# V of a batch as one 4 MB tile in 32 KB rows, P·V in four column tiles, P replicated by GpSimd, O placed by its summing matmuls, eight batches in one loop

## The chip, the cores and the metric

The kernel runs on one core of one Trainium2 chip. The metric is the device time of one execution in microseconds (us); lower is better. Executions of the kernel before agree within 0.3%: 193.13 to 193.42 us in its first three runs.

"Packet" below means one contiguous row that one of the core's 16 DMA engines moves. Each has a start and a duration in the trace, and where the text gives packet durations they are medians or means over such records. In profile lines PE is TensorE, PEld its weight loads, DVE VectorE, ACT ScalarE, POOL GpSimd and SP SyncE; a q behind a name is that engine's sequencer, and L595 is line 595 of the kernel. The trace does not say which of the 16 engines moved a packet.

## The reference

One decode step of a transformer block for 8 batches. Layernorm, a query of 32 heads of 128, attention over the last 2048 positions of a K and V cache with 8 KV heads (four query heads share one), an output projection and a residual, then an MLP block with its own layernorms.

```python
W = min(4096, max(256, Sk // 4))                       # 2048
q = (x @ wq).reshape(B, Sq, Hq, Dh).transpose(0, 2, 1, 3)
k = jnp.repeat(k_cache[:, :, Sk - W:, :], rep, axis=1)  # rep = 4
v = jnp.repeat(v_cache[:, :, Sk - W:, :], rep, axis=1)
scores = jnp.einsum("bhqd,bhkd->bhqk", q, k) * (Dh ** -0.5)
p = _softmax(scores, axis=-1)
o = jnp.einsum("bhqk,bhkd->bhqd", p, v)
return o.transpose(0, 2, 1, 3).reshape(B, Sq, Hq * Dh) @ wo
# ... then h = x + attention, and h + MLP(h)
```

All values are bf16. K and V of one batch are 4.19 MB each (8 heads x 2048 positions x 128 x 2 bytes), 67.1 MB for eight batches; the weights bring the total to 79.2 MB, each byte read once.

## The kernel before

K and V come in tiles of four KV heads (`GL = 4`). With `C = 64`, a tile's partition 4p+g (one of the 128 rows of the memory on the chip) holds 64 positions of head g: one row of 16 KB. A transfer is 32 x 4 rows, 2 MB. All transfers of K, V and weights are issued in order by SyncE.

```python
# [cut] one transfer a tile, K and V alike
src = cache[b, GL * gq:GL * (gq + 1), W0:SK, :].rearrange("g (p c) d -> p g (c d)", c=C)
e.dma_start(dst, src).then_inc(sem_slot[slot], 16)      # dst: one slot of 128 partitions x 16 KB
```

TensorE transposes K (64 groups of 16), multiplies by q, ScalarE takes the exponential in two halves, P is transposed in 16 matmuls a batch and masked. Then P·V runs in two column tiles of 64, each matmul 512 columns wide and covering four quarters of the positions at once, so that VectorE has to pick and add the quarters:

```python
        def pe_PV(e, v, parts=(0, 1)):
            # [cut] waits
            vq = slots[:, slot, :].rearrange("p (q c d) -> p c q d", q=NT, d=DH)
            for cc in range(CC):
                # [cut]
                a = cc % 2
                ins = e.matmul(pv_ps[gq][64 * a:64 * (a + 1), :].rearrange("p (q d) -> p q d", d=DH),
                               pT_sb[:, gq, cc, :], vq[:, cc, :, :],
                               start=(cc < 2), stop=(cc >= CC - 2),
                               tile_position=(0, 64 * a), skip_group_check=True)

        def dve_O1(e, v):
            # [cut]
            w = mrl[:, b % 2, gq, :]
            ins = e.tensor_scalar(o_sum[:, gq, :], pv_ps[gq][:, 0:DH], w[:, 0:1], None, ALU.mult)
            for q in range(1, NT):
                chain(e, ins, "dve_self", dve_self)
                ins = e.scalar_tensor_tensor(o_sum[:, gq, :], pv_ps[gq][:, q * DH:(q + 1) * DH], w[:, q:q + 1],
                                             o_sum[:, gq, :], ALU.mult, ALU.add)
```

## Time and profile before

| | before |
|---|---|
| time, median of 3 runs | 193.36 us |
| span of the profiled run | 191.5 us |
| PE, DVE, ACT busy | 76%, 55%, 47% |
| bytes moved | 79.3 MB |
| DMA rate in the middle of the run | about 431 GB/s |

The slice rows of the page cut the span into 40 equal parts. A digit of `DMA` is the busy share of the 16 DMA engines in tenths, and the row below is what they moved:

```profile
DMA  6999999999999999999999999999999999999991
GB/s 221 438 431 428 428 421 431 433 431 424 431 428 428 435 431 438 431 428 431 426 428 438 431 435 430 428 431 428 428 438 431 431 431 431 431 431 401 418 398 54
```

From the second slice to the last but one the engines move 398 to 438 GB/s. The part on the queues (packets, MB, time of the packets as a share of 16 engines' span) and the chain that ended last say the same: the last long piece of it is weights landing.

```profile
q1 hardware_dynamic: 6832, 79.18, 97.5%
...
DMA 11%; SPq 3%; PE 1%; DVEq 0%; DVE 0%; issue 0%
```

97.5% of 191.5 us is 186.7 us: each of the 16 engines spent that long on its packets, on average. Rows of 16 KB (K, V) took 611 ns in the median, rows of 32 KB (wq) 1213 ns: the same rate.

The groups that the change touches (busy us, mean ns of one, then the idle time before them and what ended it) and the transfers (KB each, median us from issue to landing):

```profile
L595 PE MATMUL b<-slots,pT_sb 128*64 128x512 bf16 x128 | 16.5, 384 | 1.2 <-PEq L454 1.2
L595 PE MATMUL misc<-slots,pT_sb 128*64 128x512 bf16 x128 | 15.3, 382 | 0.6 <-PEq L454 0.6
L577 DVE TENSOR_TENSOR pT_sb<-kT_ps,maskT 128x1024 bf16<-128x1024 bf16 x16 | 10.5, 685 | 10.7 <-PE kT_ps L489 10.7
L611 DVE SCALAR_TENSOR_TENSOR o_sum<-misc,mrl,o_sum 128x128 f32<-128x128 f32 x24 | 8.4, 351 | 0.8
```

```profile
slots<-in_A_k_cache_dram SPq DMA_DIRECT2D x16, 2048.0 KB, 14.2
slots<-in_A_v_cache_dram SPq DMA_DIRECT2D x16, 2048.0 KB, 16.5
slots<-in_A_wq_dram SPq DMA_DIRECT2D x1, 4096.0 KB, 12.3
```

### The profile page before, as it was taken

The page shows a single profiled execution, that of the slowest core. Times are in us where ns is not written, and L with a number is a line of the kernel's source. Part 1 is how long each engine was busy: PE and PEld are TensorE (multiplying, and loading weights), DVE is VectorE, ACT ScalarE, POOL GpSimd, SP SyncE. Part 2 cuts the span into 40 slices and gives each one's busy share as a digit, 9 for nine tenths or more (in the row PEclk, how much of TensorE's full clock was granted, in tenths as well). Part 3 has the DMA queues.
Part 4 walks back from the last instruction along what each step waited for, and adds up shares of the span by engine and source line. Part 5 has one row for each costly group of instructions (what it writes and reads, how often), then busy time and mean ns, then how long its engine had stood idle before and what let it go on. Part 6 is the DMA issues. An engine that isn't in the chain of part 4 may idle for free. (4 is left out here: it accounts for less than half of the span.)

```text
span 191.5 us, 4850 instructions
## 1 busy us (share of the span) xinstructions
PE 145.9 (76%) x2028; PEld 99.3 (52%) x2028; DVE 105.2 (55%) x287; ACT 90.3 (47%) x113; POOL 1.9 (1%) x14
## 2 busy tenths in 40 slices
PE   2027998796899869886989688968896888776854
PEld 0003876582857455645564547553655465343842
DVE  6401757464268474747474747565665657585141
ACT  3301676862656265536643564447344835406041
POOL 4000000000000000000000000000000000000000
PEclk9999999999699999999999999999999999999555
DMA  6999999999999999999999999999999999999991
GB/s 221 438 431 428 428 421 431 433 431 424 431 428 428 435 431 438 431 428 431 426 428 438 431 435 430 428 431 428 428 438 431 431 431 431 431 431 401 418 398 54
DMA packets 6857, 79.31 MB, mean 414 GB/s; under 512 B 688, under 2 KB 704, under 8 KB 2368
## 3 DMA queue, kind: packets, MB, share of 16 engines
q1 hardware_dynamic: 6832, 79.18, 97.5%
q8 instruction: 6, 0.10, 0.2%
q14 instruction: 3, 0.02, 0.0%
q10 hardware_dynamic: 16, 0.01, 0.0%
HBM read 79.18 MB, written 0.01 MB: 414 GB/s over the span
## 5 line engine op out<-in xcount | busy, mean ns | idle before, releaser
L496 ACT ACTIVATE kT_sb<-kT_ps 128x1024 bf16<-128x1024 bf16 x64 | 64.6, 1028 | 67.3 <-PE kT_ps L473 66.9
L473 PE MATMUL kT_ps<-perm_b,slots 128*128 128x128 bf16 x1024 | 68.5, 223 | 22.9 <-PEq L454 22.8
L473 PEld LDWEIGHTS kT_ps<-perm_b,slots 128*128 128x128 bf16 x1024 | 60.8, 100 | 33.7 <-issue 33.7
L500 DVE COPY kT_sb<-kT_ps 128x1024 bf16<-128x1024 bf16 x64 | 43.3, 688 | 27.1 <-PE kT_ps L473 27.1
L516 PE MATMUL S_ps<-kT_sb,qcur 128*32 128x512 bf16 x256 | 22.5, 387 | 0.8 <-PEq L454 0.8
L546 ACT ACTIVATE P_sb<-S_ps,mtile 128x1024 bf16<-128x1024 f32 x16 | 17.8, 1115 | 2.6 <-DVE mtile L537 2.5
L595 PE MATMUL b<-slots,pT_sb 128*64 128x512 bf16 x128 | 16.5, 384 | 1.2 <-PEq L454 1.2
L577 DVE TENSOR_TENSOR pT_sb<-kT_ps,maskT 128x1024 bf16<-128x1024 bf16 x16 | 10.5, 685 | 10.7 <-PE kT_ps L489 10.7
L595 PE MATMUL misc<-slots,pT_sb 128*64 128x512 bf16 x128 | 15.3, 382 | 0.6 <-PEq L454 0.6
L526 DVE TENSOR_REDUCE mtile<-S_ps 128x1 f32<-128x512 f32 x8 | 5.5, 692 | 13.6 <-PE S_ps L516 13.6
L595 PEld LDWEIGHTS misc<-slots,pT_sb 128*64 128x64 bf16 x128 | 6.8, 109 | 8.4 <-issue 3.6
L595 PEld LDWEIGHTS b<-slots,pT_sb 128*64 128x64 bf16 x128 | 6.2, 109 | 9.2 <-issue 5.7
L516 PEld LDWEIGHTS S_ps<-kT_sb,qcur 128*32 128x32 bf16 x256 | 5.3, 93 | 8.3 <-issue 4.2
L489 PEld LDWEIGHTS kT_ps<-ident_b,P_sb 128*128 128x128 bf16 x128 | 7.2, 98 | 4.1 <-issue 4.1
L489 PE MATMUL kT_ps<-ident_b,P_sb 128*128 128x128 bf16 x128 | 8.7, 219 | 0.6 <-PEq L454 0.6
L611 DVE SCALAR_TENSOR_TENSOR o_sum<-b,mrl,o_sum 128x128 f32<-128x128 f32 x24 | 8.4, 351 | 0.8
L611 DVE SCALAR_TENSOR_TENSOR o_sum<-misc,mrl,o_sum 128x128 f32<-128x128 f32 x24 | 8.4, 351 | 0.8
L395 PE MATMUL S_ps<-slots,xlnT 128*8 128x512 bf16 x32 | 3.6, 626 | 5.7 <-DMA slots<-in_A_wq_dram 5.7
L412 DVE TENSOR_SCALAR q_sb<-S_ps 128x512 bf16<-128x512 f32 x1 | 0.7, 692 | 9.1 <-PE S_ps L395 9.1
L626 DVE CAST o_all<-misc 16x128 bf16<-16x128 f32 x7 | 2.0, 279 | 6.4 <-PE misc L620 6.3
L395 PEld LDWEIGHTS S_ps<-slots,xlnT 128*8 128x8 bf16 x32 | 1.0, 117 | 7.4 <-issue 7.4
L657 ACT ACTIVATE opl<-kT_ps 128x224 bf16<-128x224 f32 x1 | 1.2, 1182 | 6.6 <-PE kT_ps L649 6.6
(104 smaller groups left out, 82.5 us busy)
## 6 DMA issues: line engine op xcount, KB each, us to landing
slots<-in_A_k_cache_dram SPq DMA_DIRECT2D x16, 2048.0 KB, 14.2
slots<-in_A_v_cache_dram SPq DMA_DIRECT2D x16, 2048.0 KB, 16.5
slots<-in_A_wq_dram SPq DMA_DIRECT2D x1, 4096.0 KB, 12.3
slots<-in_A_wo_dram SPq DMA_DIRECT2D x1, 2048.0 KB, 30.7
slots<-in_B_w_dram SPq DMA_DIRECT2D x2, 896.0 KB, 32.0
slots<-in_A_wo_dram SPq DMA_DIRECT2D x1, 1024.0 KB, 32.5
slots<-in_A_wo_dram SPq DMA_DIRECT2D x2, 512.0 KB, 33.7
slots<-in_B_w_dram SPq DMA_DIRECT2D x1, 1024.0 KB, 25.7
```

The lines of the kernel that those rows point to most:

```text
L395: ins = e.matmul(S_ps[32 * j:32 * j + B, k, :], xlnT[:, kc * B:(kc + 1) * B], wq_v[:, kc, n0:n0 + 512], start=(kc == 0), stop=(kc == KC - ...
L473: ins = e.matmul(kT_ps[t % 2][:, c * 128:(c + 1) * 128], src[:, c * 128:(c + 1) * 128], perm_b[:, :], is_transpose=True)
L489: ins = e.matmul(kT_ps[half][:, c * 128:(c + 1) * 128], P_sb[:, half * W // 2 + c * 128:half * W // 2 + (c + 1) * 128], ident_b[:, :], is_ ...
L496: e.activation(kT_sb[:, i % NKT, 0:W // 2], kT_ps[i % 2][:, 0:W // 2], ACT.Copy).then_inc(sem_Elo, 1)
L500: e.tensor_copy(kT_sb[:, i % NKT, W // 2:W], kT_ps[i % 2][:, W // 2:W]).then_inc(sem_Ehi, 1)
L516: ins = e.matmul(S_ps[32 * gl:32 * (gl + 1), 0, :], qcur[:, GL * gq + gl, o:o + 32], kv[:, gl, :, :], start=(t == 0), stop=(t == 2 * NT - ...
L526: ins = e.tensor_reduce(mtile[:, 2, 0:1], S_ps[:, 0, :], AX.X, ALU.max)
L546: e.activation(P_sb[:, half * W // 2:(half + 1) * W // 2].rearrange("r (k g) -> r k g", g=GL), s_rep, ACT.Exp, bias=mtile[:, j, 0:1], scal ...
L577: e.tensor_tensor(pT_sb[:, :, half * hc:(half + 1) * hc, :].rearrange("p a c (g x) -> p (c g) a x", g=GL), kT_ps[half][:, 0:W // 2].rearra ...
L595: ins = e.matmul(pv_ps[gq][64 * a:64 * (a + 1), :].rearrange("p (q d) -> p q d", d=DH), pT_sb[:, gq, cc, :], vq[:, cc, :, :], start=(cc < ...
L611: ins = e.scalar_tensor_tensor(o_sum[:, gq, :], pv_ps[gq][:, q * DH:(q + 1) * DH], w[:, q:q + 1], o_sum[:, gq, :], ALU.mult, ALU.add)
L626: e.tensor_copy(o_all[:, gq, b, :], pv_ps[gq][0:GL * R, OT]).then_inc(sem_oT, 1)
```

## The change

Its intent is to shorten the work behind P·V. V of a batch becomes one tile of all eight heads, partition 8p+g, rows of 32 KB (128 positions). P is replicated eight times (an exponential for two copies, GpSimd for the rest), transposed in 32 matmuls instead of 16, and masked, so that P·V runs in four column tiles of 32 and adds up the quarters by itself. One scaling replaces eight VectorE steps, and four small fp32 matmuls a batch both add up the heads and put O in place. All eight batches now run in one TensorE loop. The core of the diff:

```diff
-NS = 10
+NS = 9
+            e.memset(P_rep[:], 0.0).then_inc(sem_rep, 2)
+            for b in range(NB):                                   # GpSimd
+                e.wait_ge(sem_exp, b + 1)
+                for x in range(2):
+                    e.tensor_copy(P_rep[:, x, :]..., <P_two read four times over>).then_inc(sem_rep, 1)
 # [cut] transfers
-                if kind in "kv":
-                    b, gq = divmod(t, 2)
-                    cache = A_k_cache if kind == "k" else A_v_cache
-                    src = cache[b, GL * gq:GL * (gq + 1), W0:SK, :].rearrange("g (p c) d -> p g (c d)", c=C)
-                    e.dma_start(dst, src).then_inc(sem_slot[slot], 16)
+                if kind == "k":
+                    # [cut] as before, 32 x 4 rows of 16 KB
+                if kind == "v":
+                    if t:
+                        e.wait_ge(sem_PV, t)
+                    src = A_v_cache[t, :, W0:SK, :].rearrange("g (p c) d -> p g (c d)", c=2 * C)
+                    e.dma_start(v_loop, src).then_inc(sem_v, 16)
+                if kind == "vl":      # V of the last batch, in two halves
+                    src = A_v_cache[NB - 1, :, W0:SK, :].rearrange("g (p x c) d -> x p g (c d)", x=2, c=C)[t]
+                    e.dma_start(dst, src).then_inc(sem_vl[t], 16)
 # [cut] P·V
-                ins = e.matmul(pv_ps[gq][64 * a:64 * (a + 1), :]..., pT_sb[:, gq, cc, :], vq[:, cc, :, :], ...
-                               tile_position=(0, 64 * a), skip_group_check=True)
+                        ins = e.matmul(pv_ps[32 * q:32 * (q + 1), :],
+                                       pT_sb[:, x, c, 32 * q:32 * (q + 1)],
+                                       v[:, k * DH:(k + 1) * DH], start=(x == 0 and c == 0), stop=(x == 1 and c == CT - 1),
+                                       tile_position=(0, 32 * q), skip_group_check=True)
 # [cut] O
-            ins = e.tensor_scalar(o_sum[:, gq, :], pv_ps[gq][:, 0:DH], w[:, 0:1], None, ALU.mult)
-            for q in range(1, NT):
-                ins = e.scalar_tensor_tensor(...)
+            e.tensor_scalar(o_sum[:, :], pv_ps, rL[:, :], None, ALU.mult).then_inc(sem_O1, 1)
+                ins = e.matmul(op_ps(b), selw[:, q, :], o_sum[:, NJ * q:NJ * (q + 1)], start=(q == 0), stop=(q == 3))
 # [cut] loop
-            with e.Fori(1, NB):
+            with nc.Fori(0, NB, engines=(mybir.EngineType.PE,), head_slot={mybir.EngineType.PE: 0}):
```

## The prediction

> **What bounds the kernel now.** The transfers. The slice table shows the DMA engines 90% busy or more in 38 of 40 slices, at 421 to 438 GB/s[...]: 431 GB/s over 20 to 160 us. The chain that ended last runs over the last weight transfers (DMA 11%) and ends 3 us after the last landing, at 188 us. One batch of K and V is 8.39 MB, so 19.45 us; PE is busy 16.5 of each 20 us (stretches of 20 us). Compute matters only where it delays a transfer, or lies behind the last one.
>
> **What the change does to the bytes.** Nothing. Its 32 KB V rows may help a little: wq's 32 KB packets took 1213 ns (median), two 16 KB packets 2x611. Over seven batches that is about 0.5 us.
>
> **One batch on PE afterwards**, from durations of before (estimates):
> - Four K transposes: 4.0 us (48 matmuls took 3.02).
> - P transposes: 32 matmuls instead of 16, 2.0 us (was 1.07). The masked copy on DVE doubles to about 1.3 us each; T4 waits little for it, because QK fills the gap.
> - Sum broadcast 0.34, QK, four more transposes with QK between (1.0 + 0.33 each), the last eviction: last QK about 13.4 us after the start.
> - PV: 128 matmuls of 128 columns in four column tiles. The final product has this shape and took 1.02 us for 32 at clock 0.5, so 2 to 4 us (was 3.8).
> - O: one scaling (0.35) for eight DVE steps per batch (2.8), then four fp32 matmuls (eight passes, about 1.2 us).
> Sum 17.6 to 19.2 us: just under the 19.4 us of its transfers.
>
> GpSimd's two copies (1024 fp32 each) should take 0.9 to 1.2 us each:[...] no run has shown a copy here yet, but the 480-element memset took 0.49 us. Max, exp and copies end about 6 us after the last QK, while PE needs P some 9 us after it. Hidden, except at the end.
>
> ACT loses one exp of two (1.1 us a batch), DVE some 1 us net. None of it is critical.
>
> **Buffers.** V has one loop buffer, K two slots, so fewer transfers queue ahead. V of b+1 is issued after PV of b, about 15 us after V of b was; needed by about 18. About 3 us slack. At the start, K tile 3 waits for block 0's last transpose, near 32.5 us, as tile 2's transfer ends (about 32.2): with issue latency a gap of 1 to 2 us, once.
>
> **Tail.** The same 14.2 MB follow K tile 15. My sum puts the output projection at about 178 us (before 177.9), so last weights still end the kernel.
>
> **Time.** 193.36 - 0.5 + 1.5 = 194.4 us; 80% range 192.6 to 198.5. Faster by over 2%: 0.02; within: 0.80; slower: 0.18.
>
> **What would show it.**
> - DMA still 90% busy except a dip near 32 us; 430 GB/s after.
> - PV near 3 us a batch, about 25 ns a matmul; GpSimd copies about 1 us.
> - PE waiting on V's landing before PV, by under 1 us.
> - DVE's O accumulation gone; masked P copies near 1.3 us.
> - The last chain ending in the weights' transfers and final product.
>
> **What would make it wrong.** If a batch on PE exceeds 19.4 us (PV not overlapping, at 60 ns a matmul; slow GpSimd copies; loop overhead), V's single buffer turns the excess into DMA gaps in each of seven batches, and the tail slips: +1 us a batch would give 198 to 200. If the first gap doesn't appear, 193.

The 0.9 to 1.2 us for a GpSimd copy rests on the memset alone: 0.49 us for 480 elements gives 0.49 x 1024 / 480 = 1.05 us, an estimate from the trace before.

## The result, and the profile after

Four executions of the changed kernel took 286.81, 292.65, 290.41 and 298.59 us, median 291.53 us; the second and fourth count as slow. Executions over 1.5% slower than the fastest of the same kernel are left out of the means. The ratio of the fast runs is 1.493 (95% interval 1.477 to 1.509). Ratios in this document are the mean time of one kernel's fast runs over that of the other's of the same rounds, so not quite the ratio of the medians quoted. The profiled execution is the 286.81 us one, span 285.0 us.

The slice rows after, which answer to those of before:

```profile
DMA  7999999989999999999999999989998999999992
GB/s 295 435 430 244 285 427 225 216 179 395 304 207 189 306 389 207 199 221 425 246 202 216 363 322 202 221 278 400 205 221 205 416 258 216 205 212 274 403 411 78
```

The engines are still 90% busy in nearly every slice, but they move half as much in about half of them. "Busy" counts packets under way, not bytes. (The granted TensorE clock was lower too, 0.762 on average against 0.956. It is not taken for the cause: the lost time is found below in packets, and TensorE stood waiting for them.) The queue and the chain:

```profile
q1 hardware_dynamic: 5824, 79.18, 97.8%
...
DMA 17%; PE 2%; issue 0%; DVEq 0%; DVE 0%; another core or an unknown queue 0%
```

The same 79.18 MB took 97.8% of 285.0 us, 278.7 us of each engine, where they took 186.7 us. That is 92 us more of packet time, out of 93.5 us more span. So nearly the whole loss lies inside packets; it is not waiting between them. By row size: the 1024 packets of 32 KB (V of seven batches, and wq) had a mean of 2317 ns and a median of 2533 ns, against 1213 ns; at 611 ns for each 16 KB their excess is 70 us of every engine. The 16 KB packets (K, and V of the last batch) had a mean of 762 ns against 612, an excess of 23 us: the rows that moved beside no 32 KB row have 611 ns in the median, the K rows beside rows of V 1132, and the first half of V of the last batch, also 16 rows x 8 heads, took 1249 to 1274 ns a row (medians of 4 us) while it moved alone.

The transfers and the waits of the page and of the wait view (engine, line, what it waited for: us in total, times, longest). The last two lines are SyncE's issues of K and V:

```profile
slots<-in_A_k_cache_dram SPq DMA_DIRECT2D x16, 2048.0 KB, 24.4
slots<-in_A_v_cache_dram SPq DMA_DIRECT2D x7, 4096.0 KB, 27.5
slots<-in_A_wq_dram SPq DMA_DIRECT2D x1, 4096.0 KB, 12.4
```

```profile
PE misc L546 <- PEq L440: 86.2, 8, 13.4
```

```profile
SPq L252 <- PE kT_ps L457: 112.3, 14, 19.2
SPq L258 <- PE misc L546: 98.4, 6, 17.5
```

PE stood before P·V for 86 us in eight waits. The view names PE's own queue as the releaser, but V of one batch was issued at 100.80 us and P·V began at 128.34 us, as it landed.

The compute groups, which the prediction had sized, behaved:

```profile
L546 PE MATMUL misc<-slots,pT_sb 128*32 128x128 bf16 x1024 | 26.9, 297 | 86.2 <-PEq L440 86.2
...
L556 DVE TENSOR_SCALAR o_sum<-misc,rL 128x128 f32<-128x128 f32 x8 | 2.8, 350 | 100.7 <-PE misc L546 100.7
...
L221 POOL COPY P_rep<-P_two 128x1024 f32<-128x1024 f32 x16 | 16.2, 1040 | 222.9 <-ACT P_two L521 222.9
...
L537 DVE TENSOR_TENSOR pT_sb<-kT_ps,mask 128x2048 bf16<-128x2048 bf16 x18 | 21.3, 1220 | 6.6 <-PE kT_ps L472 6.6
```

### The profile page after: what moved, and what is told of

Same layout as the page of the kernel before. It is cut to its first block, busy times and chain, and to the rows that moved or that the text cites. A ratio compares the mean times of both kernels' runs of the same rounds, so it can differ in the third digit from the quotient of the medians.

```text
span 285.0 us, 6593 instructions
## 1 busy us (share of the span) xinstructions
PE 160.4 (56%) x2974; PEld 133.1 (47%) x2974; DVE 95.1 (33%) x192; ACT 84.5 (30%) x103; POOL 21.7 (8%) x32
## 3 DMA queue, kind: packets, MB, share of 16 engines
q1 hardware_dynamic: 5824, 79.18, 97.8%
HBM read 79.18 MB, written 0.01 MB: 278 GB/s over the span
## 5 line engine op out<-in xcount | busy, mean ns | idle before, releaser
L546 PE MATMUL misc<-slots,pT_sb 128*32 128x128 bf16 x1024 | 26.9, 297 | 86.2 <-PEq L440 86.2
L546 PEld LDWEIGHTS misc<-slots,pT_sb 128*32 128x32 bf16 x1024 | 25.0, 139 | 88.3 <-issue 88.2
L221 POOL COPY P_rep<-P_two 128x1024 f32<-128x1024 f32 x16 | 16.2, 1040 | 222.9 <-ACT P_two L521 222.9
L537 DVE TENSOR_TENSOR pT_sb<-kT_ps,mask 128x2048 bf16<-128x2048 bf16 x18 | 21.3, 1220 | 6.6 <-PE kT_ps L472 6.6
L472 PE MATMUL kT_ps<-perm_p,P_rep 128*128 128x128 bf16 x288 | 19.3, 227 | 0.0
L472 PEld LDWEIGHTS kT_ps<-perm_p,P_rep 128*128 128x128 bf16 x288 | 17.9, 103 | 1.2 <-issue 0.3
L521 ACT ACTIVATE P_two<-S_ps,mtile 128x1024 bf16<-128x1024 f32 x8 | 8.9, 1113 | 19.4 <-DVE mtile L516 19.4
L566 PE MATMUL b<-o_sum,selw 128*128 128x32 f32 x56 | 9.9, 329 | 4.3 <-PEq L440 4.3
L566 PEld LDWEIGHTS b<-o_sum,selw 128*128 128x128 f32 x56 | 9.2, 250 | 5.8 <-issue 5.8
L302 DVE TENSOR_SCALAR ident_f<-iota_f 128x128 f32<-128x128 f32 x1 | 4.8, 4791 | 1.3 <-POOL iota_f L208 1.3
```

The costliest lines, as they stand in the source:

```text
L221: e.tensor_copy(P_rep[:, x, :].bitcast(dt.float32).rearrange("r (k g) -> r k g", g=G // 2), bass.AP(tensor=two.tensor, offset=two.offset + ...
L302: e.tensor_single_scalar(ident_f[:], iota_f[:], 0.0, ALU.is_equal)
L472: ins = e.matmul(kT_ps[x][:, c * 128:(c + 1) * 128], P_rep[:, x, c * 128:(c + 1) * 128], perm_p[:, :], is_transpose=True)
L521: e.activation(P_two[:, :, :].rearrange("r x (k a) -> r x k a", a=2), bass.AP(tensor=sc.tensor, offset=0, ap=[[1024, 128], [1, 2], [2, 256 ...
L537: e.tensor_tensor(pT_sb[:, x, :, :], kT_ps[x][:, :].rearrange("p (c s) -> p c s", s=128), bass.AP(tensor=m.tensor, offset=m.offset, ap=[m. ...
L546: ins = e.matmul(pv_ps[32 * q:32 * (q + 1), :], pT_sb[:, x, c, 32 * q:32 * (q + 1)], v[:, k * DH:(k + 1) * DH], start=(x == 0 and c == 0), ...
```

## The experiments

The expectations name theories by letters. R: the read side, the addresses of V's rows in memory. W and later W': the write side. W says that the partitions which a transfer's rows go to set its rate, W' that the partitions of all the rows under way at the same moment do. Which partitions hold each other up the author assumed; no trace or run shows it. S: a row of 32 KB is slow as such. X: a DMA engine is fast only into some partitions of its own (which ones was assumed). N: a transfer of few rows is slow wherever they land. F: TensorE waits for the fetch of its own instructions (D: for data instead). All runs passed the comparison with the reference, but the inputs are so small that attention adds little to the output: the comparison also passes with V in wrong places, so where a run has wrong values the text says so.

### 1. Other source addresses

```diff
+    src = bass.AP(tensor=src.tensor, offset=src.offset,
+                  ap=[[8 * 2 * C * DH + DH, 16], [2 * C * DH, 8], [1, 2 * C * DH]])   # wrong values
     e.dma_start(v_loop, src).then_inc(sem_v, 16)
```

In the changed kernel the eight heads' rows lie 2 MB apart in memory; here they lie 32 KB apart. Everything else stays.

> Only the addresses that V is read from change (a wrong result on purpose): the same 16 by 8 rows of 32 KB into the same partitions, but rows that lie 32 KB apart instead of 2 MB, and groups of eight rows 256 KB + 256 B apart instead of 32 KB. Theory W (the slow V transfers are a matter of where rows are written[...]): no change, 32 KB packets near 2550 ns, time 285 to 300 us. Theory R (addresses 2 MB apart collide in HBM): packets back at 1213 ns, about 194 us. Theory S (a 32 KB row as such is slow): no change.

Measured: 287.72 us, V's packets still 2541 ns. R falls: the loss does not come from how far apart the rows are read.

### 2. V fetched as before, everything else changed

```diff
-    src = A_v_cache[t, :, W0:SK, :].rearrange("g (p c) d -> p g (c d)", c=2 * C)
-    e.dma_start(v_loop, src).then_inc(sem_v, 16)
+    for gq in range(2):                                    # wrong values
+        src = A_v_cache[t, GL * gq:GL * (gq + 1), W0:SK, :].rearrange("g (p c) d -> p g (c d)", c=C)
+        e.dma_start(slots[:, 2 + gq, :], src).then_inc(sem_v, 16)
```

V of the last batch likewise. The same bytes land in the same buffer, as two transfers of 32 x 4 rows of 16 KB.

> V is fetched like K, in two transfers of 32 by 4 rows of 16 KB per batch, everything else as changed (the right bytes in the wrong partitions: a wrong result on purpose). All three theories, W, R and S, expect 16 KB packets at 611 ns throughout, a V of a batch in about 9.8 us, and my own sum of the rest then 193 to 196 us. If V's transfers are not the cause, it stays near 290 us.

Measured: 196.25 us. The slices and the queue:

```profile
DMA  6999998999999999999999999999999999999990
GB/s 217 445 421 431 428 415 303 409 431 431 431 431 428 431 431 431 431 430 431 431 431 431 431 431 431 428 431 431 431 431 431 431 431 431 431 416 409 410 356 13
...
q1 hardware_dynamic: 6832, 79.18, 96.3%
```

V's 16 KB rows are back at 611 ns, and 90.6 us of the 93.5 us between the changed kernel's profiled run (286.81) and the kernel before (193.36) are gone. So the loss is the shape of V's transfers, and not GpSimd, the loop, the column tiles or the buffers. The one dip, 303 GB/s in the seventh slice, is the gap near 32 us that the prediction had: only four rows began between 31.95 and 33.27 us, and from 31 to 34 us 1.2 us of all sixteen engines' time are missing.

### 3. The opposite edit: only V's shape in the kernel before

```diff
+    if kind == "v":                                        # wrong values
+        src = cache[b, :, W0:SK, :].rearrange("g (p x c) d -> x p g (c d)", x=2, c=C)[gq]
     e.dma_start(dst, src).then_inc(sem_slot[slot], 16)
```

> The kernel before, with one edit: each of its 2 MB V tiles is fetched as 16 rows of 8 heads instead of 32 rows of 4 heads, still 16 KB rows (wrong result on purpose). Theory W: V's 16 KB packets take about 1230 to 1280 ns instead of 611, each batch needs some 29 us of transfers instead of 19.5, the kernel 262 to 278 us. If the slow V needs something else of the change (32 KB rows, GpSimd, the loop), it stays at 193 us.

Measured: 307.13 us, more than expected. From 32 us on the rate was about 210 to 310 GB/s and 73% of the 16 KB rows took over 1000 ns (median of these 1206 ns). The kernel before orders K and V tiles alternately, so K rows probably moved beside V rows most of the time and were held up too, as in the 23 us above; here K's and V's rows have one size, and the trace can't tell them apart. Run 2 shows that V's shape is needed for the loss; this one shows that it is enough for it, with rows of 16 KB and nothing else of the change. So S falls as well.

### 4. and 5. The same rows to other partitions

Eight transfers a batch, one of 16 rows for each head g: to 16 neighbouring partitions (wrong values), and, as control, to every 8th partition, which is where the changed kernel's one transfer puts them (right values).

```diff
-    e.dma_start(v_loop, src).then_inc(sem_v, 16)
+    for g in range(G):
+        e.dma_start(slots[16 * g:16 * g + 16, 2:4, :]..., src[:, g, :]).then_inc(sem_v, 16)   # v_dst_16_block
+        e.dma_start(slots[g:128:G, 2:4, :]..., src[:, g, :]).then_inc(sem_v, 16)              # v_dst_step8
```

> V's rows of one head go to 16 neighbouring partitions, in eight transfers of 16 rows of 32 KB per batch[...] (a wrong result on purpose). Theory W: [...]the packets take about twice as long again, near 4850 ns, V of a batch near 39 us, the kernel 420 to 480 us. Theory R and S: 2550 ns, 285 to 300 us.

> The control of the run before it: also eight transfers of 16 rows of 32 KB per batch, but to every eighth partition, where the changed kernel puts them; the result is right. Theory W[...], R and S all expect what the changed kernel has: packets near 2550 ns and 285 to 300 us, plus or minus what eight issues instead of one cost.

Measured: 367.84 us with V's packets at 3541 to 3713 ns (medians by batch; 4334 in the loop's last), and 298.42 us with 2527 ns. Reads and row sizes are the same in both, so the destination sets the rate. W's figure for 16 neighbours, four times 1213 (4852 ns), was the estimate; the measured packets are 2.9 to 3.1 times 1213 (3.6 in the last batch). Twice 1213 would be 2426; measured at every 8th partition 2527. The direction is right and the size for neighbours off. A reason may lie in the records: the rows begin one after another and not together (sixteen in succession take 2.6 to 4.2 us to begin, most of a row's duration), so that at most moments rows of two heads, to 32 partitions, were probably under way. That this accounts for the size was not tested.

### 6. Two issuing queues

```diff
-    e.dma_start(v_loop, src).then_inc(sem_v, 16)          # SyncE: all heads
+    for g in range(GL): e.dma_start(slots[g:128:G, 2:4, :]..., src[:, g, :]).then_inc(sem_v, 16)      # SyncE
+    for g in range(GL, G): e.dma_start(slots[g:128:G, 2:4, :]..., src[:, g, :]).then_inc(sem_v2, 16)  # ScalarE
```

If rows of heads 0 to 3 and rows of heads 4 to 7 did not hold each other up, two queues would bring back most of the rate. That they do not was the estimate; no run had shown it.

> Every V row goes where the changed kernel puts it, but heads 0-3 of a batch are fetched on the queue of SP and heads 4-7 on that of ACT, in four transfers of 16 rows each. Theory W: [...]most of the lost rate comes back: V of a batch in 10 to 14 us of transfer time, the kernel 195 to 225 us. If it is still the rows' addresses or their number per engine that limit (anything but where the rows land at one moment): no change, 285 to 300 us. The result is right.

Measured: 288.55 us (287.32 to 293.86), ratio 1.4925 (1.489 to 1.496): a miss. Sixteen packets were under way, as with one queue, V's at 2389 ns on SyncE's queue and 2334 on ScalarE's (medians): in this run the second queue did not put more packets under way. The records show a possible reason why it did not help: in the 66 us in which V moved alone and both queues had rows within 3 us, 12 or more of the rows under way belonged to one queue for 81% of the time (sixteen of SyncE's at 111 us, sixteen of ScalarE's at 113.5). The rows under way changed from one queue to the other nearly together, so that rows of the two groups of heads seldom met in equal numbers. V's rows beside which 15 or 16 belonged to one queue took 2541 ns in the median, those with 10 to 12, 2278.

### 7. Seven instead of eight

```diff
+    for g in range(G):                                     # wrong values
+        rows = slots[g:g + 106:7, 2:4, :] if g < 7 else slots[112:128, 2:4, :]
+        e.dma_start(rows..., src[:, g, :]).then_inc(sem_v, 16)
```

> Like the control with eight transfers of 16 rows per batch, but the rows of heads 0-6 go to every seventh partition instead of every eighth, and head 7's to partitions 112-127 (a wrong result on purpose). [...]Theory W: heads 0-6 fall from about 2535 ns a packet to near 1213 ns for most packets, V of a batch from 19.7 us to 11 to 15 us of transfer, the kernel to 205 to 240 us. Theory N (any transfer of 16 rows, or of 32 KB rows from scattered addresses, runs at half rate, wherever the rows land): no change, 285 to 300 us.

Measured: 303.64 us. Heads 0 to 6, on every 7th partition, took 2212 ns in the median (the middle half 2073 to 2325, the shortest 1359), and head 7, on 16 neighbours, 3762 to 4554 (medians by batch). For heads 0 to 6 that is less than step 8's 2527, but far from 1213, and the kernel is no faster than at step 8. What W expected of step 7, most packets near 1213 ns, was the estimate, and it fails here.

### 8. Eight rows at a time

Sixteen transfers of 8 rows a batch, wrong values. In the first kernel each transfer goes to every 4th partition; transfers 0 to 7 of a batch lie in partitions 0 to 63, transfers 8 to 15 in 64 to 127. In the second, twelve go to every 12th partition.

```diff
+    for n in range(2 * G):
+        s = [0, 1, 2, 3, 32, 33, 34, 35, 64, 65, 66, 67, 96, 97, 98, 99][n]
+        e.dma_start(slots[s:s + 29:4, 2:4, :]..., src[8 * (n % 2):8 * (n % 2) + 8, n // 2, :])   # v_8rows_step4
+        rows = slots[n:n + 85:12, 2:4, :] if n < 12 else slots[84 + n:84 + n + 29:4, 2:4, :]     # v_8rows_step12
```

> The changed kernel with each batch's V fetched as sixteen transfers of 8 rows of 32 KB, to every 4th partition[...] (first partition 0-3, 32-35 the lower half, then 64-67, 96-99 the upper half; values land wrongly on purpose). If 8 rows keep only 8 engines busy the total rate is low anyway, so the time is not the test (about 290 us or more); the median of the 32 KB packets is. Theory W'[...]: 1213 ns, as wq's rows. Theory X[...]: about 1213 for the lower half, clearly slower (over 1800) for the upper half. Theory N (any transfer of so few rows is slow[...]): about 2500 in both.

> As the run before, but the first twelve transfers of a batch put their 8 rows on every 12th partition[...], the last four on every 4th partition of the upper quarter; wrong values on purpose. Theory W': 1213 ns for all. Theory X: well over 1800 for the rows at step 12. Theory N: about 2500.

Measured: 340.43 and 375.87 us; as expected, the time is not the test. While V moved alone, 8.04 packets were under way on average (80 to 84 us of the first): these transfers of 8 rows kept about half of the 16 engines busy (52.8% over 78 to 84 us).

At other times eight packets of K were under way beside them, and so the trace holds a test that was not planned. Two windows of the same execution, in both of which 16 packets were under way, eight of V and eight of K. In 47.2 to 51.2 us V was at transfers 4 to 6 of a batch, counted from 0 (within partitions 32 to 63):

```profile
DMA packets 92, 1.51 MB, mean 377 GB/s; under 512 B 24, under 2 KB 24, under 8 KB 24
...
q1 hardware_dynamic: 92, 1.51, 92.4%
```

In 55.2 to 62.2 us it was at transfers 9 to 12 (within partitions 64 to 127):

```profile
DMA packets 86, 1.41 MB, mean 201 GB/s; under 512 B 21, under 2 KB 21, under 8 KB 21
...
q1 hardware_dynamic: 86, 1.41, 95.7%
```

In the first every V row of transfers 4 to 6 took 1213 ns, in the second those of transfers 10 to 12 took 2298 to 2518 ns. The five batches after this first one repeat it: beside eight rows of K, rows into the upper half took mostly 2000 to 2600 ns. The outcome by halves is what X had foretold, and not the 1213 ns for all that W' had. But rows of the upper half that began while no K was under way (64.9 to 67.3 us) were fast too: the twelve from 65.0 us on took 1213 to 1365 ns. So N falls (eight rows at a time are not slow), X falls (with every 12th partition, too, most rows that moved alone took 1213 to 1218 ns), and rows to the upper half were slow or fast by what else was under way. W', which looks at all the rows under way at a moment, leaves room for that. Which partitions K's rows were going to at those moments the trace doesn't show, and so neither why K slowed the rows of the upper half and not those of the lower.

A split by halves does not fit everything either. In the step-4 kernel three rows of each batch's transfer 7, the last in the lower half, took 1834 to 1991 ns in the first six batches, as transfer 8 began in the upper half. In the step-12 kernel, transfer 4 of the first batch has five rows in the lower half and three in the upper, and with K beside it all eight took 2186 to 2484 ns. No run here shows why rows of the lower half were slowed too.

### 9. Sixteen rows on every 4th partition

```diff
+    for g in range(G):                                     # wrong values
+        s = g if g < 4 else 60 + g
+        e.dma_start(slots[s:s + 61:4, 2:4, :]..., src[:, g, :]).then_inc(sem_v, 16)
```

> Eight transfers a batch of 16 rows to every 4th partition of one half of the partitions[...]; wrong values on purpose. Theory W': about 2500 ns. Theory X: [...]about half of the packets near 1213 to 1800 and half slower in each half. Theory N: about 2500. Time 285 to 310 us if the packets take 2500.

Measured: 292.83 us, packets 2512 ns in the median, with no fast half (2% of V's rows under 1800), close to the 2527 ns at step 8. X is refuted once more.

### 10. and 11. A case that could refute the rule

By now W' had been shaped on the runs it explained. So two kernels were made of which it expected opposite things. Both start from the kernel of run 2, and both fetch each V tile of the loop as four transfers of one head's 32 rows. Only the partitions differ: every 4th or 32 neighbours. Wrong values in both.

```diff
     for gq in range(2):
         # src as in run 2
-        e.dma_start(slots[:, 2 + gq, :], src).then_inc(sem_v, 16)
+        for g in range(GL):
+            e.dma_start(slots[g:128:GL, 2 + gq, :], src[:, g, :]).then_inc(sem_v, 16)              # v_32rows_step4
+            e.dma_start(slots[32 * g:32 * g + 32, 2 + gq, :], src[:, g, :]).then_inc(sem_v, 16)    # v_32rows_block
```

> The kernel of v_four_head_tiles (V in two 4-head tiles, 16 KB rows, wrong values on purpose), each V tile of the loop fetched as four transfers of one head's 32 rows to every 4th partition[...], and the same bytes in the same places as v_four_head_tiles. Theory W'[...]: V's 16 KB packets stay at 611 ns and the time at 194 to 200 us (more transfers to issue). A theory that one head at a time, or few rows, is slow: 900 to 1250 ns and over 230 us.

> As the run before in sources, rows and number of transfers, but each head's 32 rows go to 32 neighbouring partitions[...]. Theory W': V's packets about 1220 to 1260 ns, DMA near 216 GB/s in V's stretches, 265 to 295 us. A theory that 32 rows are enough for the full rate: 611 ns and 194 to 200 us.

Measured: 194.35 and 278.19 us, both within what W' said. The rates of the first, then of the second:

```profile
GB/s 220 436 436 432 432 429 402 414 432 436 429 429 432 436 415 432 432 427 436 432 432 429 425 432 436 422 429 436 429 429 432 432 429 427 436 427 401 410 391 26
...
q1 hardware_dynamic: 7504, 79.18, 97.2%
```

```profile
GB/s 305 410 427 424 334 331 211 225 242 436 221 211 216 353 332 211 215 266 422 211 221 209 386 299 218 218 280 408 211 213 218 394 289 215 216 303 424 410 339 7
...
q1 hardware_dynamic: 7504, 79.18, 96.7%
```

The same sources, rows, row size and number of transfers; 84 us lie between them. V's rows took 611 ns in the first and about 1180 to 1290 ns in the second (medians of stretches of 4 us). V's stretches in the second run moved 209 to 225 GB/s, and the slices of the changed kernel in which V moved alone 189 to 221.

### 12. What was left of the 194: four-head tiles again, TensorE's stalls, and the first gap

Run 2 ended 3 us after the kernel before. Its chain that ended last (start us, length us, what), where "issue" is time in which PE waited for nothing that the profile shows:

```profile
176.21 0.49 PE misc L567 x3
176.71 2.61 issue
179.32 1.18 PE misc L567 x5
...
181.15 3.27 PE S_ps L677 x119
184.42 0.83 issue
```

An instruction transfer of 16 KB began at 177.07 us. Theory F: PE had run out of instructions and waited for this transfer. Moving the loop's head by 64 instruction slots (`head_slot` from 0 to 64, nothing else) should move the stalls:

> The run with V in two four-head tiles, with the loop's first instruction 64 slots further on[...]. That run's tail shows PE idle for 2.6 us, with nothing awaited, amid the last output matmuls, while a 16 KB instruction transfer runs. Theory F (PE waits for its next block of instructions): the stall moves some 32 matmuls earlier, into the last PV, and the kernel stays within 1 us of 196.25. Theory D (it waits for data or for a semaphore that the profile doesn't show): the stall stays where it is.

Measured: 193.91 us. The stall before the end of the projection came after 87 matmuls instead of 119, 32 earlier, and the other one moved by the same 32 into P·V of the last batch:

```profile
177.85 2.41 PE S_ps L677 x87
180.26 1.71 issue
181.97 1.27 PE S_ps L677 x41
```

The stalls sit at a fixed instruction count, as F said. They are not removed by this edit. The 2.3 us less in time, outside the 1 us that was expected, is not their doing: the stalls of the tail sum to 3.4 us in run 2 and 3.6 us here, but P·V of the last batch began at 171.2 us instead of 173.4. In this execution the gap near 32 us did not appear.

That gap was tried by itself, by fetching V of batch 0 ahead of K tile 3:

```diff
-    order = [("k", 0), ("k", 1), ("vl", 0)]
-    for b in range(NB - 1):
+    order = [("k", 0), ("k", 1), ("vl", 0), ("k", 2), ("v", 0), ("k", 3)]
+    for b in range(1, NB - 1):
```

> The run with V in two four-head tiles, with V of batch 0 fetched ahead of K tile 3, so that a transfer is always queued while K tile 3 waits for PE. If the dip to 303 GB/s near 32 us is that wait, as predicted (about 1.7 us lost), it goes, and the kernel falls from 196.25 to 194 to 195 us; if the dip only moves (K tile 3 late makes K tile 5 late), it stays at 196. Wrong result on purpose, like that run.

Measured: 200.3 us (199.68 to 201.35), ratio 1.035: a miss. The gap moved to 51.6 to 58.4 us and grew to about 5 us without transfers, which fits that K tile 3 was needed sooner than V (argued, not tested). The kernel of run 2 was then repeated, with three rounds:

> The run with V in two four-head tiles once more (196.25 us in its one execution), timed, on the chip of these runs: if the gap near 32 us depends on the clock that PE is granted in the first transposes, executions spread between 194 and 196.5 us; if it is the kernel's own, all lie within 0.5 us of 196.2.

Measured: 195.31 us (194.0 to 196.22), ratio 1.008 (1.003 to 1.013). So single times of 193.9 and 196.25 lie at the ends of one spread, and the run with the moved loop head and run 2 differ no more than two executions of one kernel. The kept traces show what the gap goes with: from 17 to 22 us, around the first transposes of K, TensorE did 40 to 42 matmuls in the three profiled executions with a gap near 32 us (this one, run 2, and the second kernel of run 13) and 66 to 70 in the three without (the moved loop head, run 10, and the first kernel of run 13). The profile records no granted clock for that time in the former (its first record begins at 22.1 to 22.7 us, in the latter at 16.5 to 16.7), so that the clock is the reason, as the expectation had it, fits but is not shown.

### 13. The change without the shape, with right values

The rest of the change can be had with V in two four-head tiles: P copied four times instead of eight, 16 P transposes, P·V of each tile into its own columns, eight placing matmuls. That its values are right where attention counts was checked off the chip, by the author's word.

```diff
-        P_rep = sb([128, 2, CT * 128], dt.bfloat16, "P_rep")
+        P_rep = sb([128, 2, CT // 2 * 128], dt.bfloat16, "P_rep")
-        selw = sb([128, 4, 128], dt.float32, "selw")
+        selw = sb([128, 2, 4, 128], dt.float32, "selw")
-        o_sum = sb([128, DH], dt.float32, "o_sum")
+        o_sum = sb([128, 2, DH], dt.float32, "o_sum")
 # [cut] transfers as in run 2, P·V and placing for two tiles; the second kernel also has head_slot 64
```

> A kernel with the right result and every part of the change but its V tile: V of a batch comes in two tiles of four heads (32 by 4 rows of 16 KB), P is copied four times instead of eight and transposed by 16 matmuls instead of 32, PV writes 128 columns per group of four heads, and eight matmuls place O. Expected: transfers at 430 GB/s throughout, GpSimd's copies about 0.55 us each, the masked P copies 0.69 us, tail on PE about 2 us shorter than in the run with eight-head P; 192.8 to 195.5 us. If the first K transposes run at the low clock, a gap near 32 us costs up to 2 us, as in that run.

> The same with the loop's first instruction 64 slots further on[...]: PE's stalls on instructions in the tail move 32 matmuls earlier. 192.8 to 195.5 us, within 1 us of the run without that shift.

Measured: 194.71 us (193.53 to 196.2), ratio 1.0087 (1.0046 to 1.0128), and 196.35 us (195.35 to 198.51, the longest slow), ratio 1.0146 (1.0093 to 1.0199), above the expected 195.5. In the first's profiled run the row medians were 611 and 1213 ns again. Neither beats the kernel before, whose DMA engines were busy for 97.5% of its span: there is little left that shorter compute could win. No version found here beats it.

## Why the prediction was wrong, point by point

- **What bounds the kernel: right.** It was bound by the transfers before, and after.
- **"What the change does to the bytes. Nothing. Its 32 KB V rows may help a little": wrong, and this is the step that failed.** Number and size of the bytes did not change, but their rate did. The prediction took 1213 ns for a 32 KB row from wq, which is 128 rows to 128 partitions. V's transfer is 16 x 8 rows, and its rows took 2539 ns in the median, not 1213. Run 5, which writes the same partitions with one transfer for each head g, 16 rows to partitions 8p+g, has nearly the same durations (2527 ns); fetched as 32 x 4 rows (run 2), V's 16 KB rows took 611 ns. At the full rate and at half of it, V's 896 rows of 32 KB and 256 of 16 KB differ by (896 x 1213 + 256 x 611) / 16 = 77.7 us, an estimate from the durations before. The packets' measured excess was 93 us; the rest fell on K rows that moved beside V's.
- **The mechanism is shown as far as this:** the destination partitions alone make 84 us (194.35 and 278.19 us, runs 10 and 11), and rows to the same half of the partitions are slow or fast by what else is under way (2298 to 2518 ns or 1213 to 1365, run 8). Which partitions slow each other, and by what, is not shown: the trace names neither the engine nor the partition of a packet. So why rows at step 7 took 2212 ns, and rows of the lower half up to 2484 in the step-12 kernel, stays open, and so does 3.6 us for 16 neighbours.
- **Compute of a batch: right.** P·V took 2.4 to 3.6 us a batch, mostly 3.60 (2 to 4 predicted), GpSimd's copies 1040 ns (0.9 to 1.2 us), the masked copy 1220 ns (about 1.3 us), the scaling 350 ns (0.35 us), the placing 1.05 us in four batches and 1.9 in three (about 1.2 us). The last Q·K began 12.5 to 14.9 us after the start of a block (13.4).
- **"PE waiting on V's landing before PV, by under 1 us": wrong,** up to 13.4 us each, 86 us in all. It follows from the failed step; with four-head tiles (run 2) the DMA row has no dip after the first gap.
- **The first gap, 1 to 2 us near 32 us: right,** 1.2 us in run 2, though not in every execution.
- **Tail: right in kind, off in one term.** With four-head tiles (run 2) the projection began near 181 us instead of 178, and 2.6 us of that was PE waiting for instructions, which the prediction didn't have; in the execution without the first gap it began at 177.6, after a stall of 1.9 us.
- **The sum 194.4 us (192.6 to 198.5)** is the time of the kernel with its transfers left alone: 195.31 us for the whole change over four-head transfers, 194.71 us for the version with right values. What the prediction named as its risks (a batch on PE above 19.4 us, slow GpSimd copies, loop overhead) didn't happen.

## What to carry to other kernels

Before changing the shape of a transfer in a kernel bound by transfers, look at the order in which its rows go to the partitions, not only at which partitions the whole transfer covers: the 128 partitions in 16 x 8 order ran at half the rate of the same 128 in 32 x 4 order (189 to 221 GB/s against about 431). Take a packet's duration only from a transfer of the same shape, and look at the GB/s row beside the busy row, since the engines were busy at 90% in nearly every slice here, at the full rate and at half of it. Here, where transfers bound the kernel at their full rate, less compute bought nothing (run 13, ratio 1.0087), and a layout chosen for compute cost half of that rate while V moved.
